# A convolution fused with a two-layer MLP on one core: the start-up's loads, weight order and first transposes rearranged, and the last ten sums stored one by one

## The chip, the cores and the metric

The kernel runs on one core of one Trainium2 chip. The metric is the device time of one execution in microseconds (us), as the median of several runs. A profiled execution gives the trace; times inside it count from the first instruction of the span. TensorE is called PE, VectorE DVE, ScalarE ACT, GpSimd POOL and SyncE SP. SP and POOL issue all the DMAs here: SP those that only copy (hardware queue), POOL those that convert float32 to bfloat16 on the way (software queue).

## The reference

Each of the 192 channels of `x` (8 x 4096 x 192, float32) belongs to one of 8 heads. A causal convolution of 7 taps runs along the sequence, with softmax weights per head. Its result goes through two matrix products with a leaky ReLU between them.

```python
def _attn_ref(x, weight):
    w = weight - np.max(weight, axis=-1, keepdims=True)
    w = np.exp(w)
    w = w / (np.sum(w, axis=-1, keepdims=True) + 1e-09)
    ...
    out = np.einsum('hk,bskhg->bshg', w, x_unf)
    return out.reshape(B, S, D).astype(np.float32)

def _moe_ref(x, w_in, w_out):
    h = x @ w_in                 # 192 -> 2048
    g = np.maximum(0.01 * h, h)
    return (g @ w_out).astype(np.float32)   # 2048 -> 192
```

## The kernel before

Work goes in blocks of 512 positions of two batch rows (`e` = 0, 1) at a time; there are 32 blocks. The first five blocks are split in two halves of 256 positions, so there are ten small groups (0 to 9) and then 27 large ones (10 to 36). For each group:

- `x` is loaded, converted to bfloat16 and transposed so that channels lie on partitions: three chunks of 64 channels, the two batch rows in partitions 0-63 and 64-127. This transposed store is `xt`.
- The convolution of a group runs mostly on DVE (`conv_jobs`, L186 and L192): 21 instructions for the three chunks, accumulated into `yt`. In the program these stand one group ahead: while PE multiplies group i, DVE makes `yt` of group i + 1. For the very first half, chunks 0 and 1, and for the second half chunk 0, PE makes the convolution instead, with diagonal matrices (`pe_conv_jobs`, L211), and a scaled copy (`act_scale`, L351, on ACT) brings it to `yt`.
- `mm1` (L385) multiplies `yt` by `w_in` in units `u`; a unit is two of the 16 slices of 128 hidden columns in a small group (12 matmuls of 256 columns), one in a large group. ACT applies the leaky ReLU (L394) and writes `g`. There are two PSUM buffers `ph`, so unit u + 2 waits for ACT to have emptied unit u.
- `mm2_slot` (L413) multiplies `g` by `w_out`, one group later, and `evac_o` (L460) copies each finished sum of 128 x 192 from PSUM into `o_sb`. Every second copy is followed by a store of the pair, issued by SP (L463).

Order in the queues is written out by hand (`manual_schedule`): every engine executes in the order of the program text. What matters here is the start.

- SP issues the load of `weight` and then two loads for halves 0 and 1 of `x` (`load_first`, L118): float32, both batch rows in one DMA. A partition takes two neighbouring positions, 1536 bytes in a run.
- POOL issues four loads of `w_in` (first hidden half for `e` = 0 and 1, then second half for each; the two copies lie in the two partition halves), then half 2 of `x` into `x_rows` (L120), then `w_out` (L256) with four neighbouring rows per partition (`RUN` = 4), then half 3 in six loads (L124), then the six loads of block 2 (L78), all converting.
- Since four neighbouring rows of `w_out` lie in one partition, slice `f` of the hidden columns is not 128 neighbouring columns of `w_in` but every fourth: `lhsT` in L385 is a `DynSlice` with a step of 4. In the built program, the first four weight loads of group 0 wait each for another one of the four `w_in` loads.
- Halves 0 and 1 are converted by `cast_first` (L132): half 0 by DVE and ACT, half 1 by ACT alone, after each of the scaled copies of group 0. `transpose_first` (L148; L155 for half 2) transposes on PE and `evac_first` (L167) copies from PSUM to `xt`. The transposes of half 1 stand after unit 0 of group 0, those of half 2 after unit 6, those of half 3 in group 1 after its third step. The PE convolution for group 1 is cut into four pieces behind units 2 to 5.
- `warm` (L268) issues matmuls on zeros between the first steps.
- At the end, the last block's eight sums (`LAST` = 248 onwards) are made with full 128-row matmuls; DVE copies them and SP stores them in pairs.

Of the kernel before, what the change touches and what calls it, by code (L numbers as in the profile page):

```python
# [9 lines left out]
FP32 = mybir.dt.float32  # L10
BF16 = mybir.dt.bfloat16
# [3 lines left out]
def kernel(  # L15
# [8 lines left out]
    nc = tc.nc  # L24

    B, S, D = x.shape
# [8 lines left out]
    CH = 64  # L35
    NCH = D // CH
    ST = 512
    SUB = ST // 128
    HT = ST // 2
    HS = SUB // 2  # L40
    NFC = F // 128
    NB = S // ST
    NBLK = (B // 2) * NB
    NHALF = 5
    RUN = 4
    NPEC = 2

    const_pool = ctx.enter_context(tc.tile_pool(name="const", bufs=1))
# [51 lines left out]
    def new_xt(rp):  # L100
# [2 lines left out]

    x_half = {
        q: const_pool.tile([128, NCH, HS, 2, CH], BF16, name=f"x_half{q}") for q in (0, 1, 3)
    }  # L110
    x_rows = const_pool.tile([128, 2, HS, D], BF16, name="x_rows")

    def load_first(q):

        rows = x[0:2, q * HT : (q + 1) * HT, :].rearrange("e (p s) d -> p e (s d)", s=HS)
        if q < 2:
            x_nat[q] = stage_pool.tile([128, 2, HS, D], FP32, name="x_nat")
            nc.sync.dma_start(out=x_nat[q].rearrange("p e s d -> p e (s d)"), in_=rows)  # L118
        elif q == 2:
            nc.gpsimd.dma_start(out=x_rows.rearrange("p e s d -> p e (s d)"), in_=rows)  # L120
        else:
            for c in range(NCH):
                for e in range(2):
                    nc.gpsimd.dma_start(  # L124
                        out=x_half[q][:, c, :, e, :],
                        in_=rows[:, e].rearrange("p (s d) -> p s d", s=HS)[
                            :, :, c * CH : (c + 1) * CH
                        ],
                    )

    def cast_first(q, e, copy):
        copy(  # L132
            out=x_half[q][:, :, :, e, :],
            in_=x_nat[q][:, e, :, :].rearrange("p s (c k) -> p c s k", c=NCH),
        )

# [2 lines left out]
    def transpose_first(q):  # L139
        ts = [  # L140
            psum_o.tile([128, HS, NCH, CH], BF16, name=f"ptr{i}", tag="po") for i in range(2)
        ]
        for s in range(HS):
            for c in range(NCH):
                for i in range(2):
                    ps = slice(i * CH, (i + 1) * CH)
                    if q != 2:
                        nc.tensor.transpose(  # L148
                            out=ts[i][:, s, c, :],
                            in_=x_half[q][ps, c, s, :, :].rearrange("p e k -> p (e k)"),  # L150
                            identity=ident[ps, ps],
                        )
                        continue
                    for e in range(2):
                        nc.tensor.transpose(  # L155
                            out=ts[i][e * CH : (e + 1) * CH, s, c, :],
                            in_=x_rows[ps, e, s, c * CH : (c + 1) * CH],
                            identity=ident[ps, ps],
                        )
        ptr[q] = ts  # L160

    def evac_first(q, *copies):
        dst = xt[0][:, :, HALO + q * HT : HALO + (q + 1) * HT].rearrange(
            "p c (i k s) -> p i s c k", s=HS, i=2
        )
        for i, t in enumerate(ptr.pop(q)):
            copies[i](out=dst[:, i], in_=t)  # L167
# [78 lines left out]
    for fs in (slice(0, F // 2), slice(F // 2, F)):  # L246
        for e in range(2):
# [8 lines left out]
    nc.gpsimd.dma_start(  # L256
        out=w_out.rearrange("p (c i) d -> p c i d", i=RUN),
        in_=moe_w_out.rearrange("(c p i) d -> p c i d", p=128, i=RUN),
    )
    load_first(3)  # L260
    load_x(2)


    wa = psum_h.tile([128, 2, ST], FP32, name="warm", tag="ph")

    def warm(n, cols=HT):
        for _ in range(n):
            nc.tensor.matmul(  # L268
                out=wa[:, 0, 0:cols], lhsT=zero[:, 0:128], rhs=zero[:, 0:cols],
                start=True, stop=True,  # L270
            )


# [31 lines left out]
    select(wps_hm, slice(0, 2))  # L305
    warm(3)
    select(wps_l, 2)
    warm(7)
    warm(1, 128)
    new_xt(0)  # L310
    whm = const_pool.tile([128, NCH, 2, K + 1], FP32, name="whm")
    nc.vector.tensor_copy(out=whm, in_=wps_hm)  # L312
# [39 lines left out]
            out=out, in_=in_, func=mybir.ActivationFunctionType.Copy, scale=scale  # L352
        )

    for job in conv_jobs(groups[0], range(NPEC, NCH)):
        job()
    for c in range(NPEC):
        pe_jobs, evac_y = pe_conv_jobs(groups[0], c)
        for job in pe_jobs:
            job()  # L360
        evac_y(act_scale)
        cast_first(1, c, nc.scalar.copy)
        if c == 0:
            warm(2)


    g, po, osb, seal = {}, {}, {}, None
# [3 lines left out]
    ]  # L371
    NSUB = len(subs)
    LAST = NSUB - 2 * SUB

    def mm1(grp, u):
        blk, t0, T = grp
        y = yt[blk]
        nf = ST // T
        ph = psum_h.tile([128, 2, ST], FP32, name="ph", tag="ph")
        for i in range(nf):  # L380
            f = nf * u + i
            for c in range(NCH):
                for e in range(2):
                    ps = slice(e * CH, (e + 1) * CH)
                    nc.tensor.matmul(  # L385
                        out=ph[:, e, i * T : (i + 1) * T],
                        lhsT=w_in[
                            ps, c, bass.DynSlice(f // RUN * RUN * 128 + f % RUN, 128, RUN)
                        ],
                        rhs=y[ps, c, t0 : t0 + T],  # L390
                        start=(c == 0),
                        stop=(c == NCH - 1),
                    )
# [59 lines left out]
    def evac_o(n):  # L453
        b, e, s = subs[n]
        rp, st = divmod(b, NB)
        if n % 2 == 0:
            osb[n // 2] = o_pool.tile([128, 2, D], FP32, name="o_sb")
        o_sb = osb[n // 2]
        copy = nc.scalar.copy if b < NHALF else nc.vector.tensor_copy
        ins = copy(out=o_sb[:, n % 2, :], in_=po.pop(n))  # L460
        if n % 2 == 1:
# [5 lines left out]
        return ins  # L467

    slot, avail = 0, 0
    for i, grp in enumerate(groups):  # L470
        blk, t0, T = grp
# [91 lines left out]
```

## Time and profile before

| | us |
|---|---|
| median of 3 runs | 700.27 |
| the runs | 700.2, 700.27, 701.01 |
| the profiled execution | 701.01 |
| its span, first to last instruction | 699.3 |
| outside the span (701.01 less 699.3) | 1.7 |

The median of the runs lies 0.74 us under the profiled execution. The granted PE clock is 0.995 of full speed over the span.

| stage of the span | what runs |
|---|---|
| 0 to 15.8 | softmax weights, first half of `x`, its convolution, loading of `w_in` |
| 15.8 to 28.9 | `mm1` of group 0, halves 1 and 2 transposed |
| 28.9 to 124.8 | groups 1 to 9, `mm1` and `mm2` in turn |
| 124.8 to 685 | the large groups |
| 685 to 699.3 | the last eight sums, copies and stores |

The trace's shares of busy time are averages over these stages. What a change in one of them is worth is read from what ends last in that stage.

### The profile page before, as it was taken

What the parts mean: (1) busy time and instruction counts of PE and PEld (TensorE: products, weight loads), DVE (VectorE), ACT (ScalarE), POOL (GpSimd) and SP (SyncE); (2) the same over time, 40 slices, a digit from 0 to 9 for tenths busy, and PEclk for the clock granted to TensorE, in tenths of its full rate; (3) what the DMA queues carried; (4) which work ended last, traced back from release to release, by engine and by line L of the source; (5) the groups of instructions that cost most, each with busy time, mean ns of one, the idle gap of its engine ahead of it and who ended that gap; (6) DMA issues with size and microseconds to landing.
All of it is one profiled execution on the core that took longest, in us unless ns stands there. A gap on an engine that the chain in (4) does not pass through costs nothing.

```text
span 699.3 us, 26075 instructions
## 1 busy us (share of the span) xinstructions
PE 688.2 (98%) x11794; PEld 587.4 (84%) x11794; DVE 544.8 (78%) x1000; ACT 517.4 (74%) x578; POOL 144.3 (21%) x201
## 2 busy tenths in 40 slices
PE   6999999999999999999999999999999999999998
PEld 4799999688888888888888888888888888888887
DVE  4899999978787878887878787878887878787812
ACT  4788888977777777777777777777777777777771
POOL 6712112222221122221022222122222022000000
PEclk9899999999999999999999999999999999999999
DMA  9936555955662555554555663455654455222112
GB/s 177 96 65 84 85 77 66 100 68 74 82 91 61 81 75 74 87 84 67 79 75 71 93 81 68 83 67 73 93 80 74 78 74 66 69 60 58 47 36 69
DMA packets 182751, 53.99 MB, mean 77 GB/s; under 512 B 147824, under 2 KB 181872, under 8 KB 182640
## 3 DMA queue, kind: packets, MB, share of 16 engines
q0 software_dynamic: 98304, 14.56, 29.7%
q1 hardware_dynamic: 84336, 37.77, 22.1%
q8 instruction: 92, 1.51, 1.0%
q14 instruction: 19, 0.16, 0.1%
HBM read 29.88 MB, written 25.17 MB: 79 GB/s over the span
## 4 chain that ended last, share of the span: by engine, by line
PE 91%; DVE 5%; DMA 2%; ACT 1%; POOL 1%; issue 0%; POOLq 0%
PE po L413 46%; PE ph L385 45%; DVE yt L192 4%; DMA w_in<-in_moe_w_in_dram 2%; ACT g L394 1%; PE acc L211 0%; DVE yt L186 0%; POOL w_in L248 0%; POOL sel L238 0%; PE ptr L148 0%; POOL sel L236 0%; DVE o_sb L460 0%; ACT o_sb L460 0%; PE ptr L155 0%; POOL ident masks.py:199 0%
## 5 line engine op out<-in xcount | busy, mean ns | idle before, releaser
L394 ACT ACTIVATE g<-ph 128x1024 bf16<-128x1024 f32 x512 | 496.6, 1021 | 161.5 <-PE ph L385 161.1
L192 DVE SCALAR_TENSOR_TENSOR yt<-xt,wk,yt 128x512 bf16<-128x512 bf16 (+1 forms) x648 | 442.5, 683 | 17.7
L385 PE MATMUL ph<-yt,w_in 64*128 64x512 bf16 (+1 forms) x3552 | 387.6, 349 | 5.3 <-DMA w_in<-in_moe_w_in_dram 4.0
L413 PEld LDWEIGHTS <-g 64*128 64x128 bf16 (+1 forms) x8064 | 361.6, 94 | 33.3 <-issue 0.2
L413 PE MATMUL po<-w_out,g 64*128 64x192 bf16 (+1 forms) x8064 | 387.7, 243 | 0.0
L385 PEld LDWEIGHTS <-w_in 64*128 64x128 bf16 x3552 | 230.3, 110 | 68.6 <-DMA w_in<-in_moe_w_in_dram 4.5
L78 POOL DMA_DIRECT2D x_bf<-in_x_dram x180 | 133.8, 773 | 434.3 <-DMA xt<-x_bf 322.5
L460 DVE COPY o_sb<-po 128x192 f32<-128x192 f32 x216 | 77.1, 357 | 121.6 <-PE po L413 115.2
L186 DVE TENSOR_SCALAR yt<-xt,wk 128x512 bf16<-128x512 bf16 (+1 forms) x108 | 38.8, 359 | 1.0 <-DMA xt<-x_bf 1.0
L460 ACT COPY o_sb<-po 128x192 f32<-128x192 f32 x40 | 12.8, 320 | 1.9
L167 DVE COPY xt<-ptr 128x384 bf16<-128x384 bf16 x7 | 3.8, 583 | 7.5 <-PE ptr L148 6.3
L211 PE MATMUL acc<-xt,diag 64*64 64x256 bf16 x84 | 6.4, 284 | 0.3 <-DVE xt L167 0.3
L268 PE MATMUL warm<-zero 128*128 128x256 bf16 (+1 forms) x28 | 5.2, 340 | 1.1 <-DVE junk L228 1.1
L211 PEld LDWEIGHTS <-diag 64*64 64x64 bf16 x84 | 4.5, 109 | 1.9 <-issue 1.2
L124 POOL DMA_DIRECT2D x_half<-in_x_dram x6 | 4.3, 711 | 5.5 <-DMA w_in<-in_moe_w_in_dram 5.5
L326 ACT ACTIVATE diag<-ident,whm 128x64 bf16<-128x64 bf16 x14 | 3.5, 333 | 2.0 <-DVE whm L312 2.0
L268 PEld LDWEIGHTS <-zero 128*128 128x128 bf16 x28 | 2.9, 120 | 2.1 <-DVE junk L228 1.1
L148 PE MATMUL ptr<-ident,x_half 64*128 64x64 bf16 x36 | 1.8, 207 | 0.9 <-DVE wraw L338 0.5
L248 POOL DMA_DIRECT2D w_in<-in_moe_w_in_dram x4 | 2.6, 659 | 0.0
L148 PEld LDWEIGHTS <-x_half 64*128 64x128 bf16 x36 | 1.4, 105 | 1.4 <-ACT x_half L132 0.7
L274 ACT ACT_TABLE_LOAD x1 | 1.3, 1283 | 0.8 <-PEq L547 0.8
L351 ACT ACTIVATE yt<-acc,rsum 128x256 bf16<-128x256 f32 x3 | 1.4, 465 | 0.5 <-PE acc L211 0.5
(37 smaller groups left out, 12.7 us busy)
## 6 DMA issues: line engine op xcount, KB each, us to landing
out_dram<-o_sb SPq DMA_DIRECT2D x128, 192.0 KB, 2.1
x_bf<-in_x_dram POOLq DMA_DIRECT2D x180, 64.0 KB, 3.3
w_in<-in_moe_w_in_dram POOLq DMA_DIRECT2D x4, 384.0 KB, 8.7
xt<-x_bf SPq DMA_TRANSPOSE x90, 2.5
x_nat<-in_x_dram SPq DMA_DIRECT2D x2, 384.0 KB, 3.9
w_out<-in_moe_w_out_dram POOLq DMA_DIRECT2D x1, 768.0 KB, 14.1
x_rows<-in_x_dram POOLq DMA_DIRECT2D x1, 192.0 KB, 11.1
x_half<-in_x_dram POOLq DMA_DIRECT2D x6, 32.0 KB, 10.4
```

Source lines behind the costliest of these rows:

```text
L78: nc.gpsimd.dma_start(out=t[:, c, :, e, :], in_=src[2 * rp + e, :, :, c * CH : (c + 1) * CH],)
L124: nc.gpsimd.dma_start(out=x_half[q][:, c, :, e, :], in_=rows[:, e].rearrange("p (s d) -> p s d", s=HS)[:, :, c * CH : (c + 1) * CH],)
L167: copies[i](out=dst[:, i], in_=t)
L186: lambda s=src, d=dst, c=c: nc.vector.tensor_scalar_mul(d, s, wk[:, c, 0:1])
L192: lambda s=src, d=dst, c=c, k=k: nc.vector.scalar_tensor_tensor(out=d, in0=s, scalar=wk[:, c, k : k + 1], in1=d, op0=mybir.AluOpType.mult, ...
L211: lambda k=k, p=p, a=a, e=e, ps=ps: nc.tensor.matmul(out=acc[ps, :T], lhsT=diag[c][ps, p, k, :], rhs=xt[0][ps, c, a : a + T], start=(k == ...
L268: nc.tensor.matmul(out=wa[:, 0, 0:cols], lhsT=zero[:, 0:128], rhs=zero[:, 0:cols], start=True, stop=True,)
L326: nc.scalar.activation(out=diag[c][:, 1, k, :], in_=ident2, func=mybir.ActivationFunctionType.Copy, scale=whm[:, c, 1, k : k + 1],)
L385: nc.tensor.matmul(out=ph[:, e, i * T : (i + 1) * T], lhsT=w_in[ps, c, bass.DynSlice(f // RUN * RUN * 128 + f % RUN, 128, RUN)], rhs=y[ps, ...
L394: act = nc.scalar.activation(out=g[blk][:, nf * u : nf * (u + 1), :, t0 : t0 + T], in_=ph.rearrange("p e (i t) -> p i e t", i=nf), func=my ...
L413: return nc.tensor.matmul(out=po[m], lhsT=g[b][ps, fc, e, s * 128 : (s + 1) * 128], rhs=w_out[ps, fc, :], start=start, stop=stop,)
L460: ins = copy(out=o_sb[:, n % 2, :], in_=po.pop(n))
```

## The change

The changed kernel differs in the start and at the end.

- `w_out` is loaded with one row per partition and run (`(c p) d`), 768 bytes each; slices of `w_in` are 128 neighbouring columns. In the built program the first two weight loads of group 0 wait for the first two `w_in` loads, and unit 4 waits for the other two.
- All four halves of `x` are loaded by SP as float32, one DMA for each batch row, in runs of 768 bytes. Half 2's loads are issued when ACT has finished unit 0 of group 0, half 3's when it has finished unit 6. POOL no longer loads halves 2 and 3.
- The casts of half 1 stand on DVE inside the convolution of group 0, those of half 2 on DVE and those of half 3 on ACT (after units 2 and 3 of group 1).
- The transposes and copies of half 1 stand before group 0's first unit; those of half 2 after its last unit; those of half 3 after group 1's second step.
- The PE convolution for group 1 stands in one piece behind unit 3, its scaled copy on DVE after the last unit.
- Block 2 is loaded by POOL only after group 0's last `g` (`pjunk`).
- Two short warming matmuls, and two of 256 columns, are gone.
- The sums from number 246 on (`SINGLE`) have each a buffer and a store of their own.

```diff
-    RUN = 4
...
+    def load_first(q, after=None):
+        t = stage_pool.tile([128, 2, HS, D], FP32, name="x_nat")
+        for e in range(2):
+            ins = nc.sync.dma_start(
+                out=t[:, e, :, :],
+                in_=x[e, q * HT : (q + 1) * HT, :].rearrange("(c p) d -> p c d", p=128),
+            )
+            if after is not None and e == 0:
+                tc.add_manual_dep(ins.ins, after.ins.name,
...
-    load_first(2)
     w_out = const_pool.tile([128, NFC, D], BF16)
-    nc.gpsimd.dma_start(
-        out=w_out.rearrange("p (c i) d -> p c i d", i=RUN),
-        in_=moe_w_out.rearrange("(c p i) d -> p c i d", p=128, i=RUN),
-    )
-    load_first(3)
-    load_x(2)
+    nc.gpsimd.dma_start(out=w_out, in_=moe_w_out.rearrange("(c p) d -> p c d", p=128))
...
     warm(9)
-    warm(1, 128)
...
-    warm(7)
-    warm(1, 128)
+    warm(5)
...
-    for job in conv_jobs(groups[0], range(NPEC, NCH)):
+    for n, job in enumerate(conv_jobs(groups[0], range(NPEC, NCH))):
+        if n in (4, 5):
+            cast_first(1, n - 4, nc.vector.tensor_copy)
         job()
     for c in range(NPEC):
         pe_jobs, evac_y = pe_conv_jobs(groups[0], c)
         for job in pe_jobs:
             job()
         evac_y(act_scale)
-        cast_first(1, c, nc.scalar.copy)
         if c == 0:
             warm(2)
+    transpose_first(1)
+    evac_first(1, nc.vector.tensor_copy, nc.vector.tensor_copy)
...
+    SINGLE = LAST - 2
...
-                        lhsT=w_in[
-                            ps, c, bass.DynSlice(f // RUN * RUN * 128 + f % RUN, 128, RUN)
-                        ],
+                        lhsT=w_in[ps, c, f * 128 : (f + 1) * 128],
...
-        if n % 2 == 0:
+        if n % 2 == 0 or n >= SINGLE:
             osb[n // 2] = o_pool.tile([128, 2, D], FP32, name="o_sb")
...
+        if n >= SINGLE:
+            t0 = st * ST + s * 128
+            nc.sync.dma_start(
+                out=out_rows[2 * rp + e, t0 : t0 + 128, :], in_=osb.pop(n // 2)[:, n % 2, :]
+            )
+        elif n % 2 == 1:
...
-                mm1(grp, u)
+                act = mm1(grp, u)
                 if i == 0 and u == 0:
-                    transpose_first(1)
-                    evac_first(1, nc.vector.tensor_copy, nc.vector.tensor_copy)
...
-                if i == 0 and 2 <= u <= 5:
-                    n = len(pe_ahead) // 4
-                    for job in pe_ahead[(u - 2) * n : (u - 1) * n]:
+                if i == 0 and u == 3:
+                    for job in pe_ahead:
                         job()
-                if i == 0 and u == 5:
-                    evac_y(act_scale)
-                if i == 0 and u == 6:
-                    transpose_first(2)
+                if i == 0 and u in (0, 6):
+                    load_first(2 + u // 6, act)
+                if i == 1 and u in (2, 3):
+                    cast_first(3, u - 2, nc.scalar.copy)
...
             if i == 0 and j == 3:
+                evac_y(nc.vector.tensor_scalar_mul)
+                for e in range(2):
+                    cast_first(2, e, nc.vector.tensor_copy)
+                transpose_first(2)
                 evac_first(2, nc.vector.tensor_copy, nc.vector.tensor_copy)
+            if i == 1 and j == 1:
+                nc.gpsimd.tensor_copy(out=pjunk, in_=g[0][0:1, NFC - 1, 1, HT - 1 : HT])
+                load_x(2)
...
-            if i == 1 and j == 2:
+            if i == 1 and j == 1:
                 transpose_first(3)
                 evac_first(3, nc.vector.tensor_copy, nc.vector.tensor_copy)
```

More of the change, by code (lines that the diff above doesn't have):

```diff
@@ L102, in new_xt @@
         nc.vector.memset(xt[rp][:, :, 0:HALO], 0.0)
[L108 to L123, printed above, removed]
-                    nc.gpsimd.dma_start(
-                        out=x_half[q][:, c, :, e, :],
-                        in_=rows[:, e].rearrange("p (s d) -> p s d", s=HS)[
-                            :, :, c * CH : (c + 1) * CH
-                        ],
-                    )
+    def load_first(q, after=None):
[6 more added lines that the diff above has]
+            if after is not None and e == 0:
+                tc.add_manual_dep(
+                    ins.ins, after.ins.name,
+                    mybir.DependencyInfo(
+                        mybir.DependencyClass.Sync, mybir.DependencyReason.DATA
+                    ),
+                    reason="leave the DMA engines to the weights",
+                )
+        x_nat[q] = t
     def cast_first(q, e, copy):
+        if q % 2 == 0 and e == 0:
+            x_bf[q // 2] = xb_pool.tile([128, NCH, SUB, 2, CH], BF16, name="x_bf")
+        h = q % 2
         copy(
-            out=x_half[q][:, :, :, e, :],
+            out=x_bf[q // 2][:, :, h * HS : (h + 1) * HS, e, :],
             in_=x_nat[q][:, e, :, :].rearrange("p s (c k) -> p c s k", c=NCH),
@@ L146, in transpose_first @@
                     ps = slice(i * CH, (i + 1) * CH)
[L147 to L159, printed above, removed]
+                    nc.tensor.transpose(
+                        out=ts[i][:, s, c, :],
+                        in_=x_bf[q // 2][ps, c, (q % 2) * HS + s, :, :].rearrange(
+                            "p e k -> p (e k)"
+                        ),
+                        identity=ident[ps, ps],
+                    )
         ptr[q] = ts
@@ L163, in evac_first @@
         dst = xt[0][:, :, HALO + q * HT : HALO + (q + 1) * HT].rearrange(
-            "p c (i k s) -> p i s c k", s=HS, i=2
+            "p c (s i k) -> p i s c k", s=HS, i=2
         )
@@ L251, with warm @@
             )
-    load_first(2)
     w_out = const_pool.tile([128, NFC, D], BF16)
-    nc.gpsimd.dma_start(
-        out=w_out.rearrange("p (c i) d -> p c i d", i=RUN),
-        in_=moe_w_out.rearrange("(c p i) d -> p c i d", p=128, i=RUN),
-    )
-    load_first(3)
-    load_x(2)
+    nc.gpsimd.dma_start(out=w_out, in_=moe_w_out.rearrange("(c p) d -> p c d", p=128))
     wa = psum_h.tile([128, 2, ST], FP32, name="warm", tag="ph")
-    def warm(n, cols=HT):
+    def warm(n):
         for _ in range(n):
             nc.tensor.matmul(
-                out=wa[:, 0, 0:cols], lhsT=zero[:, 0:128], rhs=zero[:, 0:cols],
-                start=True, stop=True,
+                out=wa[:, 0, 0:HT], lhsT=zero[:, 0:128], rhs=zero, start=True, stop=True
             )
@@ L386, in mm1 @@
                         out=ph[:, e, i * T : (i + 1) * T],
-                        lhsT=w_in[
-                            ps, c, bass.DynSlice(f // RUN * RUN * 128 + f % RUN, 128, RUN)
-                        ],
+                        lhsT=w_in[ps, c, f * 128 : (f + 1) * 128],
                         rhs=y[ps, c, t0 : t0 + T],
@@ L460, in evac_o @@
         ins = copy(out=o_sb[:, n % 2, :], in_=po.pop(n))
-        if n % 2 == 1:
+        if n >= SINGLE:
+            t0 = st * ST + s * 128
+            nc.sync.dma_start(
+                out=out_rows[2 * rp + e, t0 : t0 + 128, :], in_=osb.pop(n // 2)[:, n % 2, :]
+            )
+        elif n % 2 == 1:
             t0 = st * ST + (s - 1) * 128
@@ L467, in evac_o @@
         return ins
+    pjunk = const_pool.tile([1, 1], BF16)
     slot, avail = 0, 0
```

## The prediction

> **What bounds the kernel now.** I read the page's busy times first, then busy time by stage, then the order of time on PE and DVE.
>
> ```profile
> PE 688.2 (98%) x11794; PEld 587.4 (84%) x11794; DVE 544.8 (78%) x1000; ACT 517.4 (74%) x578; POOL 144.3 (21%) x201
> ```
>
> PE is busy nearly all the span, but the stages differ (columns: stretch, its length, busy us of PE, PEld, DVE, ACT and POOL, granted PE clock, DMA share, GB/s):
>
> ```profile
> 11.00:17.00 6.00, 2.04 (x22) 1.20 (x23) 0.07 (x1) 0.88 (x2) 2.28 (x4) 0.82 1.16 206
> 17.00:22.00 5.00, 5.00 (x53) 3.03 (x48) 4.40 (x10) 3.07 (x3) 2.01 (x3) 0.53 1.24 125
> 125.00:685.00 560.00, 559.72 (x9372) 467.02 (x9368) 434.17 (x755) 419.63 (x437) 102.61 (x138) 1.00 0.50 74
> ```
>
> From 125 us PE has no gap worth naming, so only what moves the start of that stretch, or the tail behind it, moves the end. Between 11 and 17 us every compute engine stands still while DMAs run; then PE works at about half clock until 22. PE in order of time (start, length, what; in brackets the idle time before it):
>
> ```profile
> 10.92 0.30 PE L385 MATMUL ph<-yt,w_in 64*128 64x256 bf16 x1
> 11.55 0.30 PE L385 MATMUL ph<-yt,w_in 64*128 64x256 bf16 x1 [0.33 <-DMA w_in<-in_moe_w_in_dram]
> 13.79 0.30 PE L385 MATMUL ph<-yt,w_in 64*128 64x256 bf16 x1 [1.95 <-DMA w_in<-in_moe_w_in_dram]
> 15.78 1.25 PE L385 MATMUL ph<-yt,w_in 64*128 64x256 bf16 x9 [1.69 <-DMA w_in<-in_moe_w_in_dram]
> ```
>
> The first matmuls wait for one `w_in` load after another: the second had landed by 11.55, the fourth only at 15.78. Slices 0 to 7 use only the first two. Next, DVE:
>
> ```profile
> 7.97 3.09 DVE L192 SCALAR_TENSOR_TENSOR yt<-xt,wk,yt 128x256 bf16<-128x256 bf16 x6
> 17.34 1.07 DVE L167 COPY xt<-ptr 128x384 bf16<-128x384 bf16 x2 [6.28 <-PE ptr L148]
> ...
> 26.42 1.06 DVE L167 COPY xt<-ptr 128x384 bf16<-128x384 bf16 x2 [1.16 <-PE ptr L155]
> ```
>
> DVE idles 6.28 and 1.16 us. After 26.42 it works without an idle time of note (83.31 of the 89 us from 36 to 125; the rest is the short spaces between its instructions), until PE waits for it:
>
> ```profile
> 124.76 1.06 PE L385 MATMUL ph<-yt,w_in 64*128 64x512 bf16 x8 [0.75 <-DVE yt L192]
> ```
>
> So DVE's convolution chain sets when the large groups begin, PE's own chain being 0.75 us ahead of it. The price of an edit in the start is what it does to DVE's second pair of copies, now at 26.42.
>
> **The change part by part.** All starts are in us of the span.
>
> Step 1, the gate of the first unit. In the built program unit 0 now waits for the first two `w_in` loads and unit 4 for the others. The transposes of half 1 stand ahead of unit 0: PE ends the second convolution piece at 10.99, 12 transposes take 0.35 (the same at 5.95), so they end near 11.4. DVE's first convolution ended at 11.06; the two casts of half 1 inside it are 2 x 0.545 = 1.1 (L132 on DVE), so it ends at 12.2 and copies half 1 at once: 12.2 in place of 17.34, which is 5.1 earlier. The casts leave ACT, which has room there.
>
> Step 2, DVE to the second copies. From 17.34 to 25.27 DVE made two copies and 14 convolution instructions, 7.9 us; they now end at 20.1. Added: the scaled copy of 128x256 from PSUM, between the 128x192 copy (0.357) and the 128x384 copy (0.583), say 0.45; the casts of half 2, 1.1. That is 21.65. Then transposes and hand-over 0.55 (0.35, and some 0.1 on each side as between other engines): copies at 22.2, against 26.42, 4.2 earlier.
>
> Step 3, does PE let it? Unit 0's last chunk waits for DVE at 12.2; it ends at 12.8. A unit is 0.66 us (1.31 for 24 matmuls), ACT's part 1.02, two buffers: units 1 to 3 end at 13.5, 14.7 and 15.7; the undivided PE convolution, 28 matmuls in 1.7, at 17.4. Units 4 to 7, paced by ACT, end at 20.9, so the transposes at 21.7 find PE free by 0.8. Unit 4 needs the last `w_in`, 15.73 at best; half 2 (384 KB) now shares the DMA engines with it, and the two `x_nat` loads landed 1.15 us apart, so 16.9: hidden by 0.5. Half 2 is issued at 14.0; `x_nat` took 3.5 to 4.2 us to land, so 18 to 19.5 with the sharing, needed at 20.5: hidden by 1 to 2.
>
> Step 4, `w_out`. Before, it landed at 6.24 + 14.1 = 20.3, 3.7 us after `x_rows` (5.50 + 11.1 = 16.6). The new form has 2048 runs of 384 bytes written in place of 512 of 1536. No row shows that size. Lower bound 3.7 (bytes alone). Upper: the six loads of half 3, 1536 runs of 128 bytes, landed between 20.3 and 21.6 (issued 16.02, 5.6 to land), 0.83 ns a run; 2048 x 0.83 = 1.7 on top, 5.4. I take 4.5. It starts at 16.9, so it lands between 20.6 and 22.3; the first `mm2` comes at 23.4. Hidden by 1.1 at worst; each us beyond would cost PE one, after its 0.75 of slack.
>
> The Trainium skill, "DMA: Bandwidth & Descriptors", Specifications, says that transfers need 512 bytes for line rate and that smaller ones are read, modified and written. If that doubled the 3.7 us here (an estimate from the page), `w_out` would land at 24.3, 0.9 late. The 128-byte loads above moved 192 KB in 1.3 us, 150 GB/s against 210 for `w_out`: slower, but not by half.
>
> Step 5, half 3. SP issues it at 21.2 (ACT has ended unit 6); with the 64 KB loads of block 2 beside it, landing at 25 to 26. ACT casts it after units 2 and 3 of group 1: 26.5 to 28.5. Behind the casts stand ACT's next units, and behind the second the transposes on PE, which wait from 27.3 to 28.5, 1.2 (0.41 at this place before). DVE comes to its copies at 22.2 + 1.1 + 6.3 (12 instructions, 27.52 to 33.85) = 29.6: hidden by 0.6 there. PE is ready for group 2 near 34.2, DVE's `yt` at 39.3 - 4.2 = 35.1. DVE still binds, so the price is 0. Block 2's loads, now from 22.3 on, take 6 x 0.74 + 3.3 and land by 30.5; their transposes on SP stood at 42.94. Hidden by some 8 us. SP's queue holds nothing else that is due meanwhile, its first store being at 36.08.
>
> Step 6, the weight stride. A strided load takes 110 ns (L385), a plain one 94 (L413). Matmul starts follow columns alone: 24 of 256 columns take 1.31 and 32 of 192 take 1.32, that is 109 and 82.5 ns a pair, and 94 ns loads hide under 82.5. Taken: 0. If they were exposed, a gain of at most 16 ns x 1776 pairs = 28 us; the ratio of columns (1.33) to pair times (1.32) excludes most of that. Fewer warming matmuls cost nothing: they fill waits.
>
> Step 7, the tail. DVE's last copy stays where it is; the last store moves half the bytes. Its packets filled 697.1 to 697.85, 0.73 us, so 0.36 is saved (0 if the latency alone counts, 0.73 at most). Eight more issues of 0.37 fit, one per 1.32 us.
>
> Sum: -4.2 and -0.36, about -4.5. Span 699.3 - 4.5 = 694.8; that execution 701.01 - 4.5 = 696.5; on the median 700.27 - 4.5 = 695.8.
>
> **The rivals.** A, the forecast, 695.8. Step 2 may be off by 0.3 either way, step 5 cost 0.6, step 7 be off by 0.36, and two of the three runs differ by 0.07 (the third by 0.74): 695.0 to 697.1.
>
> B, PE comes too late for the transposes of half 2, because the clock falls in spite of the earlier start (PE waits for ACT between the units and for DVE at 12) or `w_in` lands late. The clock was 0.50 from 14.88 to 21.71 after a stretch of 3.41 us with 0.59 us of PE work. In the same stretch I now count some 2.2; from 4.64 to 8.06 it was 2.61 and the clock held. Price: unit 3 and the PE convolution at half speed, some 2.4, less the 0.8 of slack: -2.9 in all, 697.4, to 698.2 if two more units suffer.
>
> C, the gate does not move: the first two `w_in` loads land late, since the four `x` loads are in shorter runs. Unit 0 at 15.8 and step 3's 8.7 us behind it give transposes at 24.5, copies at 25.0, -1.4 and the tail: 698.5; with the half clock 700. Against it: the same bytes, and two landings seen by 11.55.
>
> D, slower: half 2 lands late in SP's queue behind ACT, next to the converting loads. DVE stands before its casts, and everything behind it. From 20.5 + 4.5 = 25.0 on, 11 us after its issue, the kernel is slower than before. The converting loads of half 3 did take 5.6 to 13.6; at 13.6 half 2 lands at 14.4 + 13.6 = 28.0, DVE 7.5 later than in A: 703.3. Against it: those stood behind `w_in` in POOL's own queue, while `x_nat`, in SP's, landed in 4.2 beside `w_in`.
>
> **How the numbers follow.** A 0.68, B 0.15, C 0.09, D 0.08. 0.2% (1.4 us) is about what a measurement of this kernel can tell from no change, so faster means under 698.87. A and B lie there, and a third of C: 0.86. C's rest is the same: 0.06. D is slower: 0.08. The range takes A whole, with 0.3 below it for the scatter of the runs, and B with 0.4 above: 694.7 to 698.6.
>
> **What would show it.** `L385` starting at 11.6 to 12.3 and unit 4 not waiting for `w_in`; DVE's idle 6.28 gone and its second pair of copies near 22.2; no half clock near 15; `w_out` landed by 22.3; PE's last wait for `yt` near 120.6; last store's packets in 0.37 us. Wrong if the second copies start after 24, or if PE waits for `w_out` or half 3 by more than it has slack.

## The result

| | before | after |
|---|---|---|
| median of 6 runs, us | 700.24 | 695.2 |
| lowest and highest, us | 699.61, 701.01 | 693.82, 696.42 |
| the profiled execution, us | 701.01 | 694.91 |
| its span, us | 699.3 | 693.2 |
| its granted PE clock | 0.995 | 1.0 |

After takes 0.9928 of before's time, with a 95% interval of 0.9915 to 0.9941: faster by 5.0 us, against the 4.5 forecast. The spans of the two profiled executions are 6.1 apart. The difference of 1.1 is one of sampling: the profiled run of before lay 0.77 over its median, that of after 0.29 under. So the account of the 6.1 below is one of these two executions, and not of the medians.

### The profile page after: what moved, and what is told of

It is laid out like the page before. It is cut to its first block, busy times and chain, and to the rows that moved or that the text cites. A ratio compares the mean times of both kernels' runs of the same rounds, so it can differ in the third digit from the quotient of the medians.

```text
span 693.2 us, 26064 instructions
## 1 busy us (share of the span) xinstructions
PE 684.1 (99%) x11778; PEld 539.5 (78%) x11778; DVE 544.4 (79%) x1005; ACT 516.4 (74%) x577; POOL 139.6 (20%) x195
## 4 chain that ended last, share of the span: by engine, by line
PE 93%; DMA 3%; DVE 2%; ACT 1%; POOL 0%; issue 0%; SPq 0%; POOLq 0%; DVEq 0%
PE po L392 48%; PE ph L366 45%; DVE yt L180 2%; DMA w_in<-in_moe_w_in_dram 1%; DMA x_nat<-in_x_dram 1%; DMA xt<-x_bf 1%; ACT g L373 0%; POOL sel L226 0%; DVE yt L174 0%; ACT x_bf L126 0%; POOL w_in L236 0%; PE ptr L141 0%; DVE x_bf L126 0%; SPq L447 0%; POOL sel L224 0%
## 5 line engine op out<-in xcount | busy, mean ns | idle before, releaser
L392 PEld LDWEIGHTS <-g 64*128 64x128 bf16 (+1 forms) x8064 | 352.3, 94 | 45.3 <-issue 0.2
L392 PE MATMUL po<-w_out,g 64*128 64x192 bf16 (+1 forms) x8064 | 382.7, 243 | 0.0
L366 PE MATMUL ph<-yt,w_in 64*128 64x512 bf16 (+1 forms) x3552 | 379.3, 347 | 3.1 <-DMA w_in<-in_moe_w_in_dram 1.2
L366 PEld LDWEIGHTS <-w_in 64*128 64x128 bf16 x3552 | 186.4, 94 | 98.6 <-issue 4.9
L174 DVE TENSOR_SCALAR yt<-xt,wk 128x512 bf16<-128x512 bf16 (+1 forms) x108 | 38.0, 352 | 2.1 <-DMA xt<-x_bf 2.1
L248 PE MATMUL warm<-zero 128*128 128x256 bf16 x24 | 5.1, 367 | 1.1 <-DVE junk L216 1.1
L126 DVE CAST x_bf<-x_nat 128x384 bf16<-128x384 f32 x5 | 2.3, 453 | 1.5 <-DMA x_nat<-in_x_dram 1.5
L141 PE MATMUL ptr<-ident,x_bf 64*128 64x64 bf16 x48 | 1.4, 191 | 1.4 <-ACT x_bf L126 0.9
L155 DVE COPY xt<-ptr 128x384 bf16<-128x384 bf16 x7 | 2.2, 351 | 0.5 <-PE ptr L141 0.4
## 6 DMA issues: line engine op xcount, KB each, us to landing
w_out<-in_moe_w_out_dram POOLq DMA_DIRECT2D x1, 768.0 KB, 16.5
```

The source lines that it names most:

```text
L141: nc.tensor.transpose(out=ts[i][:, s, c, :], in_=x_bf[q // 2][ps, c, (q % 2) * HS + s, :, :].rearrange("p e k -> p (e k)"), identity=ident ...
L174: lambda s=src, d=dst, c=c: nc.vector.tensor_scalar_mul(d, s, wk[:, c, 0:1])
L248: nc.tensor.matmul(out=wa[:, 0, 0:HT], lhsT=zero[:, 0:128], rhs=zero, start=True, stop=True)
L366: nc.tensor.matmul(out=ph[:, e, i * T : (i + 1) * T], lhsT=w_in[ps, c, f * 128 : (f + 1) * 128], rhs=y[ps, c, t0 : t0 + T], start=(c == 0) ...
L392: return nc.tensor.matmul(out=po[m], lhsT=g[b][ps, fc, e, s * 128 : (s + 1) * 128], rhs=w_out[ps, fc, :], start=start, stop=stop,)
```

## The profile after

The page's busy times after: PE's share is 99% in place of 98%. DVE's work is the same, and the weight loads (PEld) fell by 48 us, which moved nothing, as step 6 said: PE's lead over before is 5.56 at the second pair of hidden slices of group 11 (143.65 before, 138.09 after) and 5.57 at the last copy of the kernel.

```profile
PE 684.1 (99%) x11778; PEld 539.5 (78%) x11778; DVE 544.4 (79%) x1005; ACT 516.4 (74%) x577; POOL 139.6 (20%) x195
```

By stage (stretch, length, busy us of PE, PEld, DVE, ACT and POOL, granted clock, DMA share, GB/s):

```profile
11.00:17.00 6.00, 4.27 (x76) 3.20 (x74) 5.61 (x15) 3.90 (x5) 0.00 (x0) 1.00 1.29 199
17.00:22.00 5.00, 4.39 (x82) 3.40 (x80) 3.07 (x7) 3.60 (x5) 0.00 (x0) 1.00 0.85 152
125.00:685.00 560.00, 559.46 (x9357) 427.74 (x9353) 431.70 (x756) 414.08 (x431) 99.76 (x135) 1.00 0.49 74
```

Where 11 to 17 had been a hole for every compute engine, DVE now works 5.61 of the 6 us and PE twice what it did. The clock stays at 1.00 where it had been 0.53. The large stage is unchanged. PE after, in order of time:

```profile
11.25 0.27 PE L366 MATMUL ph<-yt,w_in 64*128 64x256 bf16 x1
12.71 1.48 PE L366 MATMUL ph<-yt,w_in 64*128 64x256 bf16 x23 [1.19 <-DMA w_in<-in_moe_w_in_dram]
...
19.92 1.75 PE L366 MATMUL ph<-yt,w_in 64*128 64x256 bf16 x24 [0.46 <-ACT g L373]
21.74 0.35 PE L141 MATMUL ptr<-ident,x_bf 64*128 64x64 bf16 x12
...
28.43 0.35 PE L141 MATMUL ptr<-ident,x_bf 64*128 64x64 bf16 x12 [0.86 <-ACT x_bf L126]
```

One wait for `w_in` is left, for the second load, and the waits until 15.78 are gone. DVE after:

```profile
11.55 0.61 DVE L155 COPY xt<-ptr 128x384 bf16<-128x384 bf16 x2
...
20.02 0.42 DVE L126 CAST x_bf<-x_nat 128x384 bf16<-128x384 f32 x1 [0.69 <-DMA x_nat<-in_x_dram]
21.25 0.43 DVE L126 CAST x_bf<-x_nat 128x384 bf16<-128x384 f32 x1 [0.81 <-DMA x_nat<-in_x_dram]
22.12 0.62 DVE L155 COPY xt<-ptr 128x384 bf16<-128x384 bf16 x2 [0.44 <-PE ptr L141]
```

The idle 6.28 is gone. In its place DVE waits 0.69 and 0.81 for half 2 of `x`, which the prediction had called hidden. Two copies take 0.61 together where they took 1.07. The second pair starts at 22.12 in place of 26.42, 4.30 earlier.

The gain grows behind that point, then shrinks. DVE's first instruction for a group of 512 positions starts at 103.67 after and at 109.66 before: 5.99 earlier, so 1.69 more than the 4.30. Before, and then after:

```profile
109.66 0.35 DVE L186 TENSOR_SCALAR yt<-xt,wk 128x512 bf16<-128x512 bf16 x1
```

```profile
103.67 0.35 DVE L174 TENSOR_SCALAR yt<-xt,wk 128x512 bf16<-128x512 bf16 x1
```

Of that 1.69, 0.88 is two pairs of copies, each 0.44 shorter (0.62 for 1.06), and 0.59 is tensor-scalar instructions (L186 before, L174 after) that took 0.4 to 0.66 instead of the usual 0.28: four before (0.55, 0.66, 0.59, 0.57 us), three after (0.58, 0.52, 0.40). The rest, 0.22, is in small spaces. PE's wait of 0.75 for DVE at the first large group is gone: PE's own work there comes 5.35 earlier (118.03 for 123.38) and DVE's `yt` 5.99, so the two now meet.

```profile
118.03 1.78 PE L366 MATMUL ph<-yt,w_in 64*128 64x512 bf16 x12
```

Then comes a wait that had been small. DVE after, around group 11:

```profile
120.78 0.35 DVE L174 TENSOR_SCALAR yt<-xt,wk 128x512 bf16<-128x512 bf16 x1 [2.06 <-DMA xt<-x_bf]
```

Before, the same instruction waited less:

```profile
125.67 0.35 DVE L186 TENSOR_SCALAR yt<-xt,wk 128x512 bf16<-128x512 bf16 x1 [0.96 <-DMA xt<-x_bf]
```

The DMA transposes of block 6 stand in SP's queue where the program text puts them, halfway through group 9; DVE now arrives sooner and waits for them. PE passes a part of it on:

```profile
135.91 1.04 PE L366 MATMUL ph<-yt,w_in 64*128 64x512 bf16 x8 [0.34 <-DVE yt L180]
```

From there to the tail PE runs 5.57 ahead of before. At the end, the last copy starts at 690.28 and the span ends 2.9 later, against 695.85 and 3.45 before: another 0.53. Together 4.30 + 1.69 - 0.42 + 0.53 = 6.10, the difference of the spans.

## The experiments

The theory: the only thing worth time is that unit 0 no longer waits for all of `w_in`. First rival: the gain is spread over the loads in rows, the plain weights, the early casts and the single stores. Second rival: the half clock of before was a large part. All ratios are to before, run on the same chip beside the kernel, with 95% intervals.

| run | median, us | before there | ratio | span, us |
|---|---|---|---|---|
| split_w_in | 694.87 | 699.85 | 0.9926 [0.9915, 0.9938] | 693.2 |
| plain_w | 694.30 | 699.85 | 0.9922 [0.9909, 0.9934] | 693.3 |
| after_gate | 699.91 | 699.85 | 1.0004 [0.9993, 1.0016] | 697.9 |
| after_pairs | 695.78 | 699.85 | 0.9937 [0.9925, 0.9949] | 694.1 |
| before_warm | 698.82 | 700.19 | 0.9983 [0.9974, 0.9992] | 697.1 |
| split_rows | 695.12 | 700.19 | 0.9926 [0.9913, 0.9938] | 692.5 |
| split_rows_single | 694.93 | 700.19 | 0.9918 [0.9904, 0.9931] | 693.2 |
| after_early_x | 695.41 | 700.19 | 0.9924 [0.9912, 0.9937] | 692.7 |
| after_again | 695.07 | 700.34 | 0.9926 [0.9912, 0.9939] | 693.3 |
| after_early_tr | 694.39 | 700.34 | 0.9920 [0.9907, 0.9932] | 693.0 |
| plain_w_single | 695.13 | 700.34 | 0.9929 [0.9917, 0.9942] | 693.4 |
| best | 694.13 | 700.34 | 0.9909 [0.9895, 0.9922] | 692.3 |

**split_w_in: before, with nothing changed but the gate.** `w_in` lies in two tiles, one for each half of the hidden columns. The stride of four stays, and so does everything else.

```diff
-    w_in = const_pool.tile([128, NCH, F], BF16)
+    w_in = [const_pool.tile([128, NCH, F // 2], BF16, name=f"w_in{h}") for h in range(2)]
...
-                out=w_in[e * CH : (e + 1) * CH, :, fs],
+                out=w_in[h][e * CH : (e + 1) * CH, :, :],
...
-                        lhsT=w_in[
-                            ps, c, bass.DynSlice(f // RUN * RUN * 128 + f % RUN, 128, RUN)
+                        lhsT=w_in[f // (NFC // 2)][
+                            ps, c,
+                            bass.DynSlice(f % (NFC // 2) // RUN * RUN * 128 + f % RUN, 128, RUN),
```

> The kernel before with w_in in two tiles, so that the first units wait only for the first two loads; stride of four, loads of x and w_out, order of transposes and pairs of stores all stay. Theory 'gate' (the gain came from the first units no longer waiting for all of w_in): first matmul with all it needs near 11.6, half 1's copies on DVE near 13 in place of 17.34, the second copies near 21 in place of 26.42, 694.5 to 696. Rival 'loads and order' (the gain came from the new x loads, casts and places of the transposes): 700.2, within 0.5. Rival 'stride' (the strided weights cost): 699 to 700.2.

It took 0.9926, as much as after's 0.9928. Its DVE in order of time:

```profile
12.82 1.06 DVE L167 COPY xt<-ptr 128x384 bf16<-128x384 bf16 x2 [1.67 <-PE ptr L148]
...
20.91 1.07 DVE L167 COPY xt<-ptr 128x384 bf16<-128x384 bf16 x2
```

The idle 6.28 shrank to 1.67 and the second pair has no wait left; it starts at 20.91, earlier than after's 22.12. In before, slices 0 to 7 never read the second half of `w_in`. Here the step is still there and the wait is not, so the step alone does not make it. It takes a step and one tile for all four loads.

**plain_w: before, with `w_out` in rows and the weights read without a step.** This is the change's own way of removing the gate, alone.

```diff
-        out=w_out.rearrange("p (c i) d -> p c i d", i=RUN),
-        in_=moe_w_out.rearrange("(c p i) d -> p c i d", p=128, i=RUN),
+    nc.gpsimd.dma_start(out=w_out, in_=moe_w_out.rearrange("(c p) d -> p c d", p=128))
...
-                            ps, c, bass.DynSlice(f // RUN * RUN * 128 + f % RUN, 128, RUN)
+                        lhsT=w_in[ps, c, f * 128 : (f + 1) * 128],
```

> The kernel before with w_out in short runs and w_in read without a stride, the rest as before. Theory 'gate': the same as split_w_in within 0.5, and w_out landing 0.5 to 2 later without a wait for it. Rival 'stride': more than 1 us faster than split_w_in, with mm1's matmuls closer together in the large groups.

0.9922, and 0.57 us from split_w_in, with intervals that overlap. So without the step the one tile makes no wait either: before's dependence came from the two together, a slice with a step being tied to loads of columns that it does not read. The strided read itself costs nothing that can be measured, although each of its weight loads takes 110 ns and the plain ones 94: a matmul of 256 or 512 columns covers both. Small writes cost little too (0.5 to 2 us was expected). `w_out` lands 4.1 us after `x_rows` (5.5 + 10.7 = 16.2, 6.24 + 14.1 = 20.3), against 3.8 in split_w_in (16.2 and 20.0) with the long runs.

**after_gate: after, with the gate put back.** Unit 0's first matmul waits for all four loads; the rest is after.

```diff
-            nc.gpsimd.dma_start(
+            w_load = nc.gpsimd.dma_start(
...
+            w_loads.append(w_load)
...
+                    while w_loads:
+                        sync(first, w_loads.pop(), "all of w_in first")
```

> The changed kernel with the gate put back: the first matmul waits for all four w_in loads. Theory 'gate': unit 0 near 16.6, its end of the group 8 to 9 us behind it, second copies on DVE near 25.5, 698 to 700. Rival 'loads and order': 695.2, within 0.5.

1.0004, with an interval of 0.9993 to 1.0016 (0.8 us either way): the whole gain is gone. PE and DVE of this kernel:

```profile
16.28 3.51 PE L368 MATMUL ph<-yt,w_in 64*128 64x256 bf16 x36 [4.86 <-DMA w_in<-in_moe_w_in_dram]
```

```profile
22.66 0.48 DVE L205 TENSOR_SCALAR yt<-acc,rsum 128x256 bf16<-128x256 f32 x1 [3.73 <-PE acc L199]
...
26.43 0.62 DVE L155 COPY xt<-ptr 128x384 bf16<-128x384 bf16 x2 [2.63 <-PE ptr L141]
```

The second pair is back at 26.43, where before had it at 26.42. DVE had made half 1's copies early in vain: its next inputs come from PE, and PE stood at the gate. Together with split_w_in this settles the theory. The removal of the gate alone gives the gain, and all the rest without it gives none that this interval could tell. (The gate put back is a little harder than before's: it opens at 16.28, where before's last wait for `w_in` ended at 15.78.) On top of the removal the rest gives none either: after and split_w_in have nearly the same ratio (0.9928 and 0.9926) and the same span of 693.2. After's last copy starts at 690.28, 0.57 later than split_w_in's at 689.71, and the stretch behind it is 0.57 shorter. So what after wins behind its last copy it had lost ahead of it: its second pair starts at 22.12, that of split_w_in at 20.91.

**after_pairs: after, with the last sums stored in pairs again.**

```diff
-    SINGLE = LAST - 2
+    SINGLE = NSUB
```

> The changed kernel with the last sums stored in pairs again. If single stores save what the last store's shorter transfer saves: 0.4 to 0.55 slower than the changed kernel's 695.2, all of it behind the last copy. If only latency counts: 695.2, the stretch from the last copy to the end as in the changed kernel.

0.9937 against 0.9928 for after, with intervals that overlap. The trace does tell it apart: the last copy starts at 690.55 and the span ends at 694.1, 3.6 later; in after_again 690.41 and 693.3, 2.9 later. So between these two kernels the single store is worth some 0.6 us in the span. Its own part is 0.44: 0.04 in the issue (0.372 and 0.332 us) and 0.4 from the issue to the landing, 1.6 us (median of the last stores) in place of 2.0, in every kernel with single stores. What follows the landing differs from kernel to kernel, by up to 0.4, and no run here says why: split_rows_single, plain_w_single and best, with single stores too, end 3.2 to 3.3 after their last copy, where split_rows, plain_w and split_w_in, with pairs, end 3.35 to 3.5 after theirs.

**before_warm: before, with 40 matmuls on zeros after the convolution of group 0.** PE is kept at work while it waits; the gate stays.

```diff
         if c == 0:
             warm(2)
+    warm(40)
```

> The kernel before with 40 warming matmuls (4.3 us) put between the convolution of group 0 and its first unit, where PE waits for w_in. The gate stays, the clock should not fall. Splits the loss into the wait and the half clock behind it. If the half clock was 2 us of it: second copies on DVE near 24.4 in place of 26.42, 697.5 to 698.5. If the clock is nothing: 700, within 0.5.

The ratio 0.9983 is 1.2 us, with 0.6 to 1.8 as its interval. By stretch, before and then before_warm (columns as above):

```profile
11.47:14.88 3.41, 0.59 (x2) 0.22 (x2) 0.00 (x0) 0.44 (x2) 1.43 (x2) 1.00 1.15 204
14.88:21.71 6.83, 5.93 (x62) 3.91 (x64) 4.11 (x9) 3.07 (x3) 2.57 (x4) 0.50 1.27 157
```

```profile
11.47:14.88 3.41, 3.41 (x34) 3.05 (x32) 0.00 (x0) 0.44 (x2) 1.43 (x2) 1.00 1.16 208
14.88:21.71 6.83, 6.55 (x106) 4.96 (x104) 4.97 (x11) 4.78 (x5) 2.73 (x4) 1.00 1.27 156
```

The clock holds, and half 1's copies still wait 5.39. The second pair starts as expected for a half clock worth 2 us, 1.97 before that of before:

```profile
24.45 1.06 DVE L167 COPY xt<-ptr 128x384 bf16<-128x384 bf16 x2
```

The span, 697.1, is 2.2 shorter than that of before's profiled execution. The median falls by less. The half clock seems to have two lengths: in before's profile it lasts from 14.88 to 21.71, 6.8 us, and the mean clock is 0.995; in after_gate's it lasts half as long, from about 15.7 to 19.1, and the mean is 0.998. Of 41 executions of before beside the experiments, 27 had a mean clock of 0.994 or 0.995 and a median of 700.34 us, 14 had 0.998 and 699.37; before_warm, at 0.999 to 1.0, has 698.82. So of the 5.0 that the removal of the gate gives in split_w_in, about 1.2 is the half clock that the gate had brought with it, and the rest is the gate's wait itself.

**split_rows and split_rows_single: split_w_in, with all of `x` in rows; then with single stores too.**

```diff
-        rows = x[0:2, q * HT : (q + 1) * HT, :].rearrange("e (p s) d -> p e (s d)", s=HS)
+        rows = x[0:2, q * HT : (q + 1) * HT, :].rearrange("e (s p) d -> p e s d", s=HS)
...
-            "p c (i k s) -> p i s c k", s=HS, i=2
+            "p c (s i k) -> p i s c k", s=HS, i=2
```

> split_w_in with x of halves 0 to 3 taken as in the changed kernel, position s*128 + p in partition p, so that the copies to xt write without a stride (two loads per half and run of 768 bytes). Theory 'copies': the copies of 128x384 on DVE 0.35 in place of 0.58, DVE's chain 0.5 to 0.9 shorter, 0.2 to 0.6 faster than split_w_in (694.9). Rival: shorter runs delay w_in by 0.5 or more and take it back: 694.9 or slower, w_in's second load past 11.9.

> split_rows with the last ten sums stored by themselves. 0.4 to 0.6 faster than split_rows, all of it after the last copy: 693.8 to 694.3.

0.9926 and 0.9918; split_w_in had 0.9926. Neither edit moves the median by more than its interval, though a copy that writes without a step takes 0.35 instead of 0.58 us here. With the shorter runs the second `w_in` load came later (PE waited for it until 11.58 in split_rows and 12.37 in split_rows_single, and not at all in split_w_in), which may have given back a part; that was not tried by itself. The 0.4 to 0.6 expected of the single stores did not show. These two are inconclusive for the small terms.

**after_early_x: after, with half 2 of `x` loaded as soon as its buffer is free.** It tests what the waits 0.69 and 0.81 cost.

```diff
     load_first(1)
+    load_first(2)
...
-                if i == 0 and u in (0, 6):
+                if i == 0 and u == 6:
```

> The changed kernel with half 2 loaded as soon as its buffer is free, near 6, and not after unit 0. If its late landing costs (DVE's two idle times of 0.69 and 0.81 before the casts): these gone, second copies at 21 to 21.6. Against that w_in shares the DMA engines with it: its loads land 1 us later, unit 0 starts near 13.7 and PE reaches the transposes of half 2 near 22.5, so the copies come at 23 and it is as slow or up to 0.8 slower than 695.2. I expect the second.

Its DVE:

```profile
19.24 0.74 DVE L126 CAST x_bf<-x_nat 128x384 bf16<-128x384 f32 x2
21.36 0.62 DVE L155 COPY xt<-ptr 128x384 bf16<-128x384 bf16 x2 [1.38 <-PE ptr L141]
```

The waits for half 2 are gone, and 1.38 us of waiting for PE stands in their place: PE ends unit 7 only then. The copies start 0.76 earlier, 0.50 of which is the second `w_in` load, which here came at 12.21 instead of 12.71. So the second case, in which the load was to come 1 us later and the copies at 23, did not come true. The time is the same, 0.9924. The late half 2 cost about 0.3 at most.

**after_again and after_early_tr: after once more, and after with the DMA transposes of block 6 issued a step earlier in group 9.**

```diff
-            if j == steps // 2 and last_half and blk > 0:
+            if j == steps // (4 if blk == NHALF - 1 else 2) and last_half and blk > 0:
```

> The changed kernel once more, to stand beside the next three on the same chip: 694.9 to 695.6.

> The changed kernel with the DMA transposes of block 6 issued one step earlier in group 9. In the changed kernel DVE waited 2.06 us for them before group 11's convolution, and PE then 0.34 for DVE. If that is where 0.4 of the gain was given back: DVE's wait gone, 0.3 to 0.5 faster than after_again. If not: the same, with the wait in another place.

DVE at group 11, after_again and then after_early_tr:

```profile
114.40 4.69 DVE L180 SCALAR_TENSOR_TENSOR yt<-xt,wk,yt 128x512 bf16<-128x512 bf16 x6
120.94 0.35 DVE L174 TENSOR_SCALAR yt<-xt,wk 128x512 bf16<-128x512 bf16 x1 [1.85 <-DMA xt<-x_bf]
```

```profile
114.38 4.69 DVE L180 SCALAR_TENSOR_TENSOR yt<-xt,wk,yt 128x512 bf16<-128x512 bf16 x6
118.98 0.35 DVE L174 TENSOR_SCALAR yt<-xt,wk 128x512 bf16<-128x512 bf16 x1
```

The wait is gone, and with it PE's short one behind it, after_again first:

```profile
135.33 1.75 PE L366 MATMUL ph<-yt,w_in 64*128 64x512 bf16 x12
```

```profile
135.31 1.48 PE L366 MATMUL ph<-yt,w_in 64*128 64x512 bf16 x12
```

The traces show 0.3 us won; the medians differ by 0.68, within the intervals.

**plain_w_single and best.** The first is plain_w with single stores. The second adds the earlier transposes and halves 2 and 3 of `x` in rows, so that their copies write without a step; halves 0 and 1 keep their long runs.

```diff
-            "p c (i k s) -> p i s c k", s=HS, i=2
+            "p c (i k s) -> p i s c k" if q < 2 else "p c (s i k) -> p i s c k", s=HS, i=2
```

> plain_w with the last ten sums stored by themselves, that is the kernel before with only w_out's layout, the stride and the tail changed. 0.4 to 0.6 faster than plain_w (694.3): 693.6 to 694.3, and 0.5 to 1.5 faster than after_again.

> plain_w_single with x of halves 2 and 3 in rows, so that their copies to xt write without a stride (DVE's 128x384 copies 0.35 in place of 0.58), and block 6's DMA transposes one step earlier. In plain_w PE waited 1.15 us for DVE at group 10; with DVE 0.9 ahead that wait goes down to 0.2 to 0.4: 0.4 to 0.9 faster than plain_w_single. If PE's own chain binds instead: the same as plain_w_single.

plain_w_single came out 0.8 us above plain_w, within the intervals, and level with after_again; 0.4 to 0.6 under plain_w and 0.5 to 1.5 under after_again had been expected. PE waited 0.79 for a late second `w_in` load in it. best has the lowest median, 694.13, and the shortest span, 692.3. Its DVE shows both kinds of copy in one kernel:

```profile
12.47 1.05 DVE L171 COPY xt<-ptr 128x384 bf16<-128x384 bf16 x2 [1.15 <-PE ptr L152]
...
20.20 0.61 DVE L171 COPY xt<-ptr 128x384 bf16<-128x384 bf16 x2
```

Its second pair starts at 20.20, 1.9 before after's. It is 1.0 us under plain_w_single, a little more than expected, but not in the expected way: PE's wait for DVE at group 10 is 0.80 here and 0.70 there, and not 0.2 to 0.4, because PE's own work came 1.18 earlier and DVE's `yt` 1.08. It is 0.94 us under after_again, though the intervals of the two ratios overlap; all four of its runs lie under all five of after_again. It beats before clearly and after probably.

## Why the prediction was right, step by step

The likeliest case came true: the time, 695.2, lies 0.6 under the forecast of 695.8 and inside its range of 694.7 to 698.6. The mechanism, the gate ahead of unit 0, is shown from both sides. Several sizes were off, and two of them cancelled. In the terms of the sum, the span of a profiled execution, 4.5 was forecast and 6.1 came, so the sum was 1.6 too small. That the median fell by 5.0 only, and so came nearer to the forecast, is luck in which executions were profiled.

**Step 1, the gate.** Half 1's copies start at 11.55; 12.2 was forecast, because the casts were priced at 0.545 each. They took 0.42, and they cost less than they took:

```profile
8.14 1.52 DVE L180 SCALAR_TENSOR_TENSOR yt<-xt,wk,yt 128x256 bf16<-128x256 bf16 x3
9.58 0.42 DVE L126 CAST x_bf<-x_nat 128x384 bf16<-128x384 f32 x1
9.92 0.47 DVE L180 SCALAR_TENSOR_TENSOR yt<-xt,wk,yt 128x256 bf16<-128x256 bf16 x1
10.30 0.42 DVE L126 CAST x_bf<-x_nat 128x384 bf16<-128x384 f32 x1
10.64 0.99 DVE L180 SCALAR_TENSOR_TENSOR yt<-xt,wk,yt 128x256 bf16<-128x256 bf16 x2
```

Each row starts 0.08 to 0.09 before the one ahead of it has ended. The convolution with both casts inside takes 3.80 (7.83 to 11.63), without them 3.40 in before (7.66 to 11.06): 0.2 a cast. The row I used was the first cast of the kernel, at 5.26; that same cast takes 0.58 in after too, and the later ones 0.42. One instruction is a thin base for a price. The first unit itself was late: its wait ended at 12.71, past the 11.6 to 12.3 named as a sign.

**Step 2, the second copies.** 22.2 was forecast and 22.12 measured, but the agreement is partly luck. DVE was ready for half 2's casts at 19.33, not 20.55, since copies and casts are shorter. Then it waited 1.5 for half 2. The term of the sum, 4.2, was the right size for this point and too small for what follows: at the first group of 512 positions it is 5.99. The shorter copies (0.88) were missed outright. Before's `evac_first` writes every second element (`p c (i k s)`, with `s` innermost), after's writes neighbours. The Trainium skill, "VectorE: DVE Perf Modes", section "What auto-detection actually checks", says that the fast mode for 16-bit data needs a step of one. Our rows agree, 0.583 us with a step of two and 0.351 without. I had not laid that rule beside the change.

**Step 3, does PE let it?** PE was ready for the transposes at 21.67, 0.8 later than forecast, since the second `w_in` load came at 12.71 (rival C's cause, in small). PE's last wait for `yt`, forecast near 120.6, is gone there and comes at 135.91 instead. Half 2, "hidden by 1 to 2", landed late; its last piece was cast from 21.25. It cost little, as after_early_x shows, because PE and half 2 became ready at the same time.

**Step 4, `w_out`.** Landed at 5.51 + 16.5 = 22.0, inside 20.6 to 22.3, and PE did not wait for it. By plain_w, the writes of 384 bytes alone cost 0.3 us (4.1 for 3.8). After's 5.5, from the last `w_in` at 16.5, is 1.4 more and a little over the term's upper bound of 5.4, in a stretch in which half 2's loads ran beside it. Between the same two points it is 4.5 to 4.9 in after_again, after_early_tr and after_pairs, which load alike, and 4.0 and 3.8 in after_early_x and after_gate, which issue half 2's loads earlier or later: that fits the shared DMA engines as the cause. The Trainium skill, "DMA: Bandwidth & Descriptors", Specifications, has transfers under 512 bytes read, modified and written. Had that doubled the 3.8 us it would have been an estimated 7.6. The measurement is 4.1, and it decides.

**Step 5, half 3.** PE waited 0.86 at 28.43 (1.2 forecast), which was covered, as the step said. The 0.6 by which DVE's copies were to be hidden is not there in every kernel: in after_again and after_early_x DVE waited 0.60 for these transposes.

**Step 6, the stride.** Price 0, confirmed by split_w_in against plain_w, and by PE's lead, 5.56 at group 11 and 5.57 at the end. The step also put the fewer warming matmuls at nothing, and that is not safe. PE's first convolution piece, in after and then in after_again, the same program:

```profile
7.43 1.72 PE L199 MATMUL acc<-xt,diag 64*64 64x256 bf16 x28 [0.53 <-DVE xt L155]
```

```profile
7.53 3.19 PE L199 MATMUL acc<-xt,diag 64*64 64x256 bf16 x28
```

The same 28 matmuls take nearly twice as long, though the granted clock reads 1.00 in these stretches of both profiles. So it is in three of the six profiles with after's start (after_again and after_early_tr 3.19, after_pairs 2.51) and in none of the eight with before's warming matmuls, where this piece takes 1.72 each time. In after_again half 1's copies start at 13.01 by it, and DVE's first instruction for 512 positions at 104.04 in place of 103.67. Whether the missing warming matmuls are the cause was not tried.

**Step 7, the tail.** 0.53 in the trace against 0.36, inside its bounds of 0 and 0.73. The store itself gave 0.44, near the forecast; the rest lies behind its landing and is not explained.

**What the sum lacked.** Besides the copies, the 0.42 given back at group 11: the prediction followed DVE to the wait of PE at 124.76 and didn't ask which transfer DVE would meet next.

**The rivals.** B fell: the clock held at 1.0 with 1.76 us of PE work in the stretch where before had 0.59; I had counted 2.2. The Trainium skill, "TensorE: Matmul & The Clock Gate", Part 1, has the clock halved after an idle window of about 3.4 us. Before's row, 0.59 of 3.41 us busy and then 0.50, agrees, and shows that such a window need not be wholly idle. C came true only in its first link, the late second load, and D in its own, the late half 2; neither reached its price.

## What to carry to other kernels

When an engine waits for several loads of one tile in turn, ask which of them the instruction really reads: a slice with a step may tie it to all of the tile, and two tiles untie it without moving a byte. Price a gain past the first point where it shows, up to the next transfer that the earlier engine will meet, since each of those takes some back. Two terms that cancel look like a good forecast; only the trace shows that they were both wrong.

## What was not expected of the hardware

- The half clock seems to have two lengths, 6.8 us in before's profile and about 3.4 in after_gate's, and both occur in executions of one program: the mean clock is 0.994 or 0.995 in 27 of 41 runs of before and 0.998 in 14, a difference of 1.0 us in their medians. before_warm, without it, has a spread of 1.1 us over 11 runs, before 2.7 over 15 on the same chip. But the half clock is not all of the scatter: after, at 0.997 to 1.0, has a spread of 2.6 over 6.
- The second `w_in` load ended PE's wait at times from 11.41 (best) to 13.16 (after_pairs), and in split_w_in and plain_w PE had no wait of note for it. That is as large as the small terms looked for, so medians of five runs did not separate them.
- PE's matmuls early in the kernel can run at about half speed where the granted clock reads 1.00: 28 of them in 3.19 us or in 1.72, in two executions of one program (step 6).
- A tensor-scalar instruction of 128x256 takes 0.28 us mostly, and 0.4 to 0.66 now and then in the stretch after the start. Why was not tried.
